# Four edits at once to a fused attention and feed-forward kernel: a score chunk in array quarters, a new first quad, a new order behind the row sums, new last tiles

## Chip, cores, metric

One core of one Trainium2 chip. The metric is device time of one launch in microseconds (us); the lower the better.

## The reference

Attention over 8 batches, 12 heads, 448 positions, 64 channels, all float32, with q and k normalised by row; then a feed-forward over the 3584 tokens whose nonlinearity is `h * softmax(h)`, normalised by row.

```python
q_n, k_n = rmsnorm(q, g_q), rmsnorm(k, g_k)          # x / sqrt(mean(x*x) + 1e-6) * g
attn = softmax(q_n @ k_n^T / 8)                      # rows of 448
x = (attn @ v) as [3584, 768]
h = x @ w_in                                         # [3584, 1024]
solu = h * softmax(h)
ln = (solu - mean) / sqrt(var + 1e-6) * g_ln
out = ln @ w_out                                     # [3584, 768]
```

## The kernel before

Instruction order is laid out by hand. A *pair* is two heads of one batch, a *quad* two pairs (a, b), 24 quads in all. Scores are made transposed, keys on partitions: 448 keys are three chunks of 128 and a last one of 64; the last chunks of both pairs of a quad share one tile.

```python
def scores(n, kc):                                   # chunk kc of pair n: 64 rows by 128 columns of the array
    s = ps_t.tile([P, 2, 512], FP32, tag="t", name="s")
    for h in range(2):
        hh = slice(h * D, (h + 1) * D)
        nc.tensor.matmul(s[:, h, 0:S], d["qkT"][hh, 1, kc * P : (kc + 1) * P], d["qkT"][hh, 0, :], ...)
    exponentials(d, kc, s)                           # ScalarE

def ff_max(t):                                       # maximum and exponential of h, one call
    nc.vector.tensor_reduce(nmax, d["h"], AX, OP.max, negate=True)
    ...
    nc.scalar.activation(d["u"], d["h"], AF.Exp, bias=nmax, accum_out=d["s"])

def ff_in2(t):
    ff_in(t, 1)                                      # second half of h; h has one PSUM buffer
    later(1, lambda: ff_max(t))                      # "1 unit later": behind the next piece of TensorE work
    later(2, lambda: ff_moments(t))                  # the product h*u frees h
    later(3, lambda: ff_norm(t))
... # cut: the loop over quads; its end:
            qk_transpose(b + 2)                      # VectorE, waits for GpSimd's normalised q and k
            ...
            unit(lambda: sums(m))                    # row sums by TensorE
            later(1, lambda m=m: inverse(m))         # VectorE transposes the sums, GpSimd copies reciprocals
            later(2, lambda m=m: divide(m))          # VectorE divides
```

In these traces TensorE, ScalarE and VectorE start an instruction behind those issued to them before it, so the place of an instruction in such a list is its place in a queue. From quad 6 on (`W_IN`), pieces of the feed-forward go between the score chunks; from quad 11 (`W_OUT`) eight pieces a quad.

## Time and profile before

1006.01 us, the median of three runs (1005.66 to 1008.05). I cut the span where the character changes and read each cut from the TensorE timeline: the time at which a quad's first scores start.

| | first scores | quad 1 | quad 2 (A) | quads 2–5 (B) | quads 6–10 (C) | quads 11–23 (D) | to last output matmul (E) | store |
|---|---|---|---|---|---|---|---|---|
| before | 15.52 | 37.54 | 54.44 | 63.97 | 131.87 | 606.23 | 141.86 | 6.0 |

The first three columns are points of time, the others lengths. A is the time up to the start of quad 2, D ends where the row sums of quad 23 start, and A to E and the store add up to the span of 1004.4; the time of a launch is 1.8 us longer than its span. In the prediction A ends where quad 1 starts. One line of the TensorE timeline is needed later, the first scores of quad 1 (start, duration, what they are as far as the window asked for reaches, and in brackets the idle time ahead of them and what ended it):

```profile
37.54 3.36 PE L636 MATMUL s<-qkT 64*128 64x448 f32 x8 [4.47 <-ACT qkT L622]
```

### The profile page before, as it was taken

What the parts mean: (1) busy time and instruction counts of PE and PEld (TensorE: products, weight loads), DVE (VectorE), ACT (ScalarE), POOL (GpSimd) and SP (SyncE); (2) the same over time, 40 slices, a digit from 0 to 9 for tenths busy, and PEclk for the clock granted to TensorE, in tenths of its full rate; (3) what the DMA queues carried; (4) which work ended last, traced back from release to release, by engine and by line L of the source; (5) the groups of instructions that cost most, each with busy time, mean ns of one, the idle gap of its engine ahead of it and who ended that gap; (6) DMA issues with size and microseconds to landing.
All of it is one profiled execution on the core that took longest, in us unless ns stands there. A gap on an engine that the chain in (4) does not pass through costs nothing.

```text
span 1004.4 us, 10943 instructions
## 1 busy us (share of the span) xinstructions
PE 954.0 (95%) x3699; PEld 427.7 (43%) x3699; DVE 513.7 (51%) x758; ACT 361.1 (36%) x621; POOL 296.0 (29%) x635
## 2 busy tenths in 40 slices
PE   3899999998999999999999999999999999999997
PEld 1233333332444443444444444444444444555554
DVE  3788866668452535343535453436444445454520
ACT  4777665566332322232332233223323223011110
POOL 2576633333141414131414140514233232000000
PEclk9899999999999999999999999999999999999999
DMA  7776654443130303030303030303031010534310
GB/s 158 152 158 148 137 112 103 93 92 75 33 56 17 71 16 59 12 72 16 71 16 71 15 56 19 69 16 56 20 67 34 17 35 0 195 110 144 112 53 35
DMA packets 235962, 70.11 MB, mean 70 GB/s; under 512 B 225136, under 2 KB 225144, under 8 KB 235896
## 3 DMA queue, kind: packets, MB, share of 16 engines
q1 hardware_dynamic: 228152, 57.84, 26.4%
q10 hardware_dynamic: 7744, 11.47, 3.0%
q8 instruction: 31, 0.51, 0.2%
q14 instruction: 35, 0.29, 0.1%
HBM read 58.27 MB, written 11.01 MB: 69 GB/s over the span
## 4 chain that ended last, share of the span: by engine, by line
PE 83%; DVE 6%; ACT 4%; POOL 3%; DMA 2%; SPq 1%; issue 1%; ACTq 0%; POOLq 0%; DVEq 0%
PE h L756 29%; PE po L811 28%; PE s L636 9%; PE o L689 8%; PE pu L800 2%; PE sm L713 2%; PE s L648 2%; PE o L678 2%; ACT E L629 1%; POOL qkn L608 1%; DVE qkT L618 1%; SPq L543 1%; POOL ss L582 1%; DMA v<-in_v_dram 1%; DVE w_in L482 1%
## 5 line engine op out<-in xcount | busy, mean ns | idle before, releaser
L811 PE MATMUL po<-w_out,uT 128*128 128x384 f32 x896 | 298.6, 489 | 6.7 <-DVE r L721 3.4
L756 PE MATMUL h<-w_in,xT 128*128 128x512 f32 x672 | 300.6, 597 | 0.0
L811 PEld LDWEIGHTS po<-w_out,uT 128*128 128x128 f32 x896 | 168.0, 190 | 137.4 <-issue 16.7
L756 PEld LDWEIGHTS h<-w_in,xT 128*128 128x128 f32 x672 | 124.3, 190 | 157.6 <-issue 151.3
L629 ACT ACTIVATE E<-s 128x896 f32<-128x896 f32 x168 | 149.4, 915 | 103.7 <-PE s L636 99.8
L636 PE MATMUL s<-qkT 64*128 64x448 f32 x576 | 139.7, 589 | 22.3 <-ACT qkT L622 10.7
L689 PE MATMUL o<-E,v 128*64 128x448 f32 x576 | 113.8, 544 | 1.7 <-ACT E L629 1.7
L784 POOL TENSOR_TENSOR he<-he,mhalf 128x1 f32<-128x1 f32 x28 | 17.4, 622 | 332.1 <-DVE he L783 332.1
L812 ACT COPY y<-po 128x384 f32<-128x384 f32 x56 | 26.8, 479 | 219.7 <-PE po L811 219.7
L802 DVE COPY uT<-pu 128x512 f32<-128x512 f32 x28 | 19.2, 687 | 160.2 <-PE pu L800 92.4
L668 DVE TENSOR_TENSOR es<-es,E 128x896 f32<-128x896 f32 (+1 forms) x52 | 56.5, 1087 | 75.1 <-ACT E L629 67.5
L665 POOL TENSOR_TENSOR es<-E 128x896 f32<-128x896 f32 x26 | 55.7, 2144 | 127.0 <-ACT E L629 127.0
L636 PEld LDWEIGHTS s<-qkT 64*128 64x128 f32 x576 | 48.3, 190 | 104.4 <-issue 44.3
L769 ACT ACTIVATE u<-h,hmax 128x1024 f32<-128x1024 f32 x28 | 31.2, 1113 | 154.5 <-DVE hmax L766 154.5
L608 POOL TENSOR_TENSOR qkn<-qk,ny 128x896 f32<-128x896 f32 x47 | 79.7, 1697 | 8.8 <-DVE qkT L618 3.0
L766 DVE TENSOR_REDUCE hmax<-h 128x1 f32<-128x1024 f32 x28 | 34.3, 1224 | 86.7 <-PE h L756 86.7
L618 DVE STREAM_TRANSPOSE qkT<-qkn 128x896 f32<-128x896 f32 x48 | 53.2, 1109 | 44.0 <-POOL qkn L608 44.0
L689 PEld LDWEIGHTS o<-E,v 128*64 128x64 f32 x576 | 39.1, 137 | 74.6 <-issue 67.7
L569 DVE TENSOR_REDUCE part<-sq 128x28 f32<-128x896 f32 x48 | 51.0, 1063 | 30.1 <-ACT sq L564 30.1
L600 POOL TENSOR_TENSOR nx<-nx,ny 128x28 f32<-128x28 f32 x47 | 23.9, 509 | 124.6 <-ACT ny L595 124.6
L564 ACT ACTIVATE sq<-qk 128x896 f32<-128x896 f32 x48 | 45.6, 950 | 36.8 <-DVE part L569 25.3
L582 POOL COPY ss<-part 32x28 f32<-32x28 f32 x188 | 44.4, 236 | 16.3 <-DVE part L569 7.7
(83 smaller groups left out, 710.2 us busy)
## 6 DMA issues: line engine op xcount, KB each, us to landing
qk<-in_q_dram SPq DMA_DIRECT2D x192, 56.0 KB, 2.1
out_dram<-y ACTq DMA_DIRECT2D x28, 384.0 KB, 2.3
qk<-in_k_dram SPq DMA_DIRECT2D x184, 56.0 KB, 2.2
v<-in_v_dram SPq DMA_DIRECT2D x96, 96.0 KB, 2.4
raw<-in_moe_w_in_dram SPq DMA_DIRECT2D x12, 512.0 KB, 4.5
raw<-in_moe_w_out_dram SPq DMA_DIRECT2D x16, 384.0 KB, 3.2
again<-in_moe_w_in_dram SPq DMA_DIRECT2D x13, 448.0 KB, 5.2
again<-in_moe_w_out_dram SPq DMA_DIRECT2D x13, 448.0 KB, 3.4
```

The lines of the kernel that those rows point to most:

```text
L564: nc.scalar.activation(d["sq"], d["qk"].rearrange("p s b d -> p (s b) d"), AF.Square)
L569: nc.vector.tensor_reduce(d["part"], d["sq"], AX, OP.add)
L582: first(n).tensor_copy(d["ss"][g * 32 : g * 32 + 32], d["part"][o * 32 : o * 32 + 32])
L608: first(n).tensor_tensor(d["qkn"], d["qk"].rearrange("p s b d -> p (s b) d"), d["y"].rearrange("p b -> p b ()").to_broadcast([P, 2 * NB, 32]),
L618: nc.vector.transpose(d["qkT"].rearrange("p s t -> p (s t)"), d["qkn"].rearrange("p b d -> p (b d)"))
L629: nc.scalar.activation(d["E", kc], s[:, :, 0:S], AF.Exp)
L636: nc.tensor.matmul(s[:, h, 0:S], d["qkT"][hh, 1, kc * P : (kc + 1) * P], d["qkT"][hh, 0, :], start=True, stop=True)
L665: engine.tensor_tensor(d["es"], d["E", 0], d["E", 1], OP.add)
L668: engine.tensor_tensor(d["es"][pp], d["es"][pp], x[pp], OP.add)
L689: nc.tensor.matmul(d["o"][h * D : (h + 1) * D, :], d["v"][:, h, kc], d["E", kc][:, h], start=False, stop=(kc == NJ - 1),)
L756: nc.tensor.matmul(d["h"][:, hs], xTs[m][:, c, i * P : (i + 1) * P], w_in[:, c, hs], start=(c == 0), stop=(c == KD - 1))
L811: nc.tensor.matmul(po, d["uT"][:, c], w_out[:, c, hs], start=(c == 0), stop=(c == KF - 1))
```

## The change

Its intent, by part. **Quarters:** the third chunk as four 64x64 matmuls, the mode of the matmuls that follow, so that TensorE changes its mode once less (0.19 us a change by the trace before, read from the starts). **First quad:** the gains of q and k are loaded by GpSimd's queue and made into columns on ScalarE; eight matmuls warm TensorE up; pair 2 is normalised in quad 0. **Order of h's exponential:** maximum one and exponential two units later, so that a score exponential needn't wait behind it. **Inverse at once:** the inverse of the sums directly behind them. **Last tiles:** their transposes ahead of the previous tile's second output half; the last store in halves; the check's small transposes elsewhere.

```diff
     def scores(n, kc):
-        for h in range(2):
-            nc.tensor.matmul(s[:, h, 0:S], d["qkT"][hh, 1, kc * P : (kc + 1) * P], ...)
+        w = P if kc < NJ - 1 else D
+        for c in range(0, P, w):
+            for h in range(2):
+                nc.tensor.matmul(s[c : c + w, h, 0:S], d["qkT"][hh, 1, kc * P + c : kc * P + c + w], ...)
@@ setup
+        nc.gpsimd.dma_start(gg[:, i], g_q or g_k)        # and grow: five small loads; before: SyncE, behind load(1)
@@ def gain_columns()
         nc.tensor.transpose(pg, grow, ident)
-        nc.vector.tensor_copy(gcol, pg)
+        nc.scalar.copy(gcol, pg)
@@ def ff_in2(t)
-        later(1, lambda: ff_max(t))                      # maximum and exponential
-        later(2, lambda: ff_moments(t))
-        later(3, lambda: ff_norm(t))
+        more = 0 if t >= NT - SHORT else 1               # SHORT = 8
+        later(1 + more, lambda: ff_max(t))               # maximum alone
+        later(1 + 2 * more, lambda: ff_exp(t))
+        later(2 + 2 * more, lambda: ff_moments(t))
+        later(3 + 2 * more, lambda: ff_norm(t))
@@ start
+        for _ in range(8):                               # ahead of all other TensorE work
+            nc.tensor.matmul(warm[:, 0:S], ident, q and k of pair 0, start=True, stop=True)
@@ quad 0
+                rsqrt_seed(2)                            # these three: before, in the middle of quad 1's preparation
+                rsqrt_step(2)
+                normalise(2)
@@ end of a quad
-                qk_transpose(b + 2)
             unit(lambda: sums(m))
-            later(1, lambda m=m: inverse(m))
-            later(2, lambda m=m: divide(m))
+            if a < W_IN and next1:
+                qk_transpose(b + 2)
+            inverse(m)
+            if a >= W_IN and next1:
+                qk_transpose(b + 2)
+            later(1, lambda m=m: divide(m))
... (cut: last tiles, one conversion step moved into the start, the order of the loads)
```

More of the change, by code (lines that the diff above doesn't have):

```diff
@@ L375, in fast_path @@
     out: bass.AP,
-    grow: bass.AP,
-    within: bass.AP,
+    g_q: bass.AP,
+    g_k: bass.AP,
+    moe_g_ln: bass.AP,
     large: bass.AP,
-    load_gains,
-    bound_scores,
 ):
@@ L401, in fast_path @@
     LAG = 4
+    SHORT = 8
     assert H * D == DM and 2 * D == P and NJ * P + D == S and NP % 2 == 0 and B % 2 == 0 and 2 * S % P == 0
@@ L414, in fast_path @@
     w_out = consts.tile([P, KF, DM], FP32, name="w_out")
+    grow = consts.tile([KF + 2, P], FP32, name="grow")
+    gg = consts.tile([P, 2, D], FP32, name="gg")
+    gmax = consts.tile([P, 1], FP32, name="gmax")
+    within = consts.tile([P, 1], FP32, name="within")
     gcol = consts.tile([P, KF + 2], FP32, name="gcol")
@@ L435, in setup, with gain_columns, gain_limit @@
         make_identity(nc, ident)
-    def gains():
-        bound_scores()
+        for i, g in enumerate((g_q, g_k)):
+            nc.gpsimd.dma_start(gg[:, i], g.rearrange("(o d) -> o d", o=1).to_broadcast([P, D]))
+            nc.gpsimd.dma_start(
+                grow[KF + i : KF + i + 1].rearrange("o (h d) -> o h d", h=2),
+                g.rearrange("(o d) -> o () d", o=1).to_broadcast([1, 2, D]),
+            )
+        nc.gpsimd.dma_start(grow[0:KF, :], moe_g_ln.rearrange("(c p) -> c p", p=P))
+    def gain_columns():
         pg = ps_t.tile([P, KF + 2], FP32, tag="t", name="pg")
         nc.tensor.transpose(pg, grow, ident[0 : KF + 2, 0 : KF + 2])
-        nc.vector.tensor_copy(gcol, pg)
-        nc.vector.tensor_scalar(
+        nc.scalar.copy(gcol, pg)
+        nc.gpsimd.tensor_tensor(gg[:, 0], gg[:, 0], gg[:, 1], OP.mult)
+    def gain_limit():
+        limit = 80.0 / float(D) ** 0.5
+        nc.gpsimd.tensor_scalar(large, gmax[0:1], limit, None, OP.is_gt)
+        nc.gpsimd.tensor_scalar(within, gmax, limit, float(D) ** -0.5, OP.is_le, OP.mult)
+        nc.gpsimd.tensor_scalar(
             gcol[:, KF : KF + 1], gcol[:, KF : KF + 1], gcol[:, KF + 1 : KF + 2], within, OP.mult, OP.mult
@@ L511, in check_all @@
         one = small.tile([1, 2], FP32, tag="one", name="one")
-        pw = ps_t.tile([1, 2, P], FP32, tag="t", name="pw")
+        pw = ps_h.tile([1, 2, P], FP32, tag="h", name="pw")
         nc.vector.tensor_reduce(worst[:, 0:1], extent[:, 0], AX, OP.min)
@@ L633, in scores @@
         s = ps_t.tile([P, 2, 512], FP32, tag="t", name="s")
-        for h in range(2):
-            hh = slice(h * D, (h + 1) * D)
-            nc.tensor.matmul(
-                s[:, h, 0:S], d["qkT"][hh, 1, kc * P : (kc + 1) * P], d["qkT"][hh, 0, :], start=True, stop=True
-            )
+        w = P if kc < NJ - 1 else D
+        for c in range(0, P, w):
+            for h in range(2):
+                hh = slice(h * D, (h + 1) * D)
+                nc.tensor.matmul(
+                    s[c : c + w, h, 0:S], d["qkT"][hh, 1, kc * P + c : kc * P + c + w], d["qkT"][hh, 0, :],
+                    start=True, stop=True,
+                )
         exponentials(d, kc, s)
@@ L764, in ff_max, with ff_exp @@
         d = mt[t]
-        nmax = small.tile([P, 1], FP32, tag="hmax", name="hmax")
-        nc.vector.tensor_reduce(nmax, d["h"], AX, OP.max, negate=True)
+        d["nmax"] = small.tile([P, 1], FP32, tag="hmax", name="hmax")
+        nc.vector.tensor_reduce(d["nmax"], d["h"], AX, OP.max, negate=True)
+    def ff_exp(t):
+        d = mt[t]
         d["u"] = work.tile([P, DFF], FP32, tag="u", name="u", bufs=LAG + 1)
         d["s"] = small.tile([P, 1], FP32, tag="hsum", name="hsum")
-        nc.scalar.activation(d["u"], d["h"], AF.Exp, bias=nmax, accum_out=d["s"])
+        nc.scalar.activation(d["u"], d["h"], AF.Exp, bias=d["nmax"], accum_out=d["s"])
     def ff_moments(t):
@@ L812, in ff_out @@
         nc.scalar.copy(d["y"][:, hs], po)
+        if t == NT - 1:
+            nc.scalar.dma_start(out[t * P : (t + 1) * P, hs], d["y"][:, hs])
+        elif half == 1:
+            nc.scalar.dma_start(out[t * P : (t + 1) * P, :], d["y"])
         if half == 1:
-            nc.scalar.dma_start(out[t * P : (t + 1) * P, :], d["y"])
             del mt[t]
@@ L878, in fast_path, with second @@
     waiting = []
-    def second(t, a, b):
-        return [(W_OUT, lambda: ff_transpose(t)), a, (W_OUT, lambda: ff_out(t, 0)), b, (W_OUT, lambda: ff_out(t, 1))]
-    nothing = (0, None)
+    def second(t):
+        return [
+            (W_OUT, lambda: ff_transpose(t)),
+            (W_OUT, lambda: ff_out(t, 0)),
+            (W_OUT, lambda: ff_out(t, 1)),
+        ]
     for t in range(NT):
-        ready = -(-(t + 1) * P // S) * NP
-        a = (max(ready, W_IN), lambda t=t: ff_in(t, 0))
-        b = (max(ready, W_IN), lambda t=t: ff_in2(t))
+        ready = max(-(-(t + 1) * P // S) * NP, W_IN)
+        a = (ready, lambda t=t: ff_in(t, 0))
+        b = (ready, lambda t=t: ff_in2(t))
         waiting.append(t)
-        if len(waiting) > (LAG if t < NT - 8 else 1):
-            c, _, d, _, e = second(waiting.pop(0), nothing, nothing)
+        if len(waiting) > (LAG if t < NT - SHORT else 1):
+            c, d, e = second(waiting.pop(0))
             events += [a, c, b, d, e]
@@ L894, in fast_path @@
     for t in waiting:
-        events += [x for x in second(t, nothing, nothing) if x[1]]
+        c, d, e = second(t)
+        if t == waiting[0]:
+            events += [c, d, e]
+        else:
+            events[-1:] = [c, events[-1], d, e]
     N = B * NP
@@ L905, in fast_path @@
     load(0)
+    setup()
     load(1)
-    load_gains()
-    setup()
+    load_next()
     load_next()
@@ L911, in fast_path @@
     load(3)
-    load_next()
     load_v(0)
@@ L915, in fast_path @@
     with tc.manual_schedule():
+        warm = ps_h.tile([P, DFF], FP32, tag="h", name="warm")
+        for _ in range(8):
+            nc.tensor.matmul(
+                warm[:, 0:S], ident, st[0]["qk"][:, 1].rearrange("p b d -> p (b d)"), start=True, stop=True
+            )
         squares(0)
@@ L922, in fast_path @@
         rsqrt_seed(0)
+        gain_columns()
+        begin(0)
         rsqrt_step(0)
-        gains()
+        nc.vector.tensor_reduce(gmax, gg[:, 0], AX, OP.max, apply_absolute_value=True)
         normalise(0)
@@ L927, in fast_path @@
         fold_sums(1)
+        gain_limit()
         rsqrt_seed(1)
@@ L932, in fast_path @@
         gain(0)
+        step(0)
+        end(0)
         at = 0
@@ L990, in fast_path @@
             if next1:
-                rsqrt_seed(a + 2)
-                rsqrt_step(a + 2)
-                normalise(a + 2)
+                if m:
+                    rsqrt_seed(a + 2)
+                    rsqrt_step(a + 2)
+                    normalise(a + 2)
                 rsqrt_seed(b + 2)
@@ L996, in fast_path @@
             if m == 0:
-                begin(0)
-                step(0)
-                end(0)
                 begin(1)
@@ L1046, in fast_path @@
             unit(f)
-            while x < len(again) and x * len(last) < (u + 1) * (len(again) + 2):
+            while x < len(again) and 5 * x < 7 * u:
                 check_w(x, raw[x])
@@ L1051, in fast_path @@
                     raw.append(load_again(x + 3))
-            if u == len(last) - 2:
-                assert x == len(again)
+            if 5 * (u - 1) == 100:
+                assert x == len(again) and u < len(last)
                 check_all()
@@ L1073 @@
     nc = tc.nc
-    D = q.shape[3]
-    P = 128
-    KF = moe_w_in.shape[1] // P
-    gains = ctx.enter_context(tc.tile_pool(name="gains", bufs=1))
-    grow = gains.tile([KF + 2, P], FP32, name="grow")
-    gg = gains.tile([P, 2, D], FP32, name="gg")
-    gmax = gains.tile([P, 1], FP32, name="gmax")
-    within = gains.tile([P, 1], FP32, name="within")
-    flag = gains.tile([1, 1], I32, name="flag")
-    large = gains.tile([1, 1], FP32, name="large")
-    def load_gains():
-        nc.sync.dma_start(grow[0:KF, :], moe_g_ln.rearrange("(c p) -> c p", p=P))
-        for i, g in enumerate((g_q, g_k)):
-            for h in range(2):
-                nc.sync.dma_start(grow[KF + i : KF + i + 1, h * D : (h + 1) * D], g.rearrange("(o d) -> o d", o=1))
-            nc.sync.dma_start(gg[:, i], g.rearrange("(o d) -> o d", o=1).to_broadcast([P, D]))
-    def bound_scores():
-        nc.gpsimd.tensor_tensor(gg[:, 0], gg[:, 0], gg[:, 1], OP.mult)
-        nc.vector.tensor_reduce(gmax, gg[:, 0], AX, OP.max, apply_absolute_value=True)
-        nc.gpsimd.tensor_scalar(large, gmax[0:1], 80.0 / float(D) ** 0.5, None, OP.is_gt)
-        nc.gpsimd.tensor_scalar(within, gmax, 80.0 / float(D) ** 0.5, float(D) ** -0.5, OP.is_le, OP.mult)
-    fast_path(tc, q, k, v, moe_w_in, moe_w_out, out, grow, within, large, load_gains, bound_scores)
+    flags = ctx.enter_context(tc.tile_pool(name="flags", bufs=1))
+    flag = flags.tile([1, 1], I32, name="flag")
+    large = flags.tile([1, 1], FP32, name="large")
+    fast_path(tc, q, k, v, moe_w_in, moe_w_out, out, g_q, g_k, moe_g_ln, large)
     nc.vector.tensor_copy(flag, large)
```

## The prediction

> **What bounds the kernel now.** I read the busy shares, then a table by stage (cut where the profile changes character), TensorE's waits, the chain of waits and the engines' timelines inside each stage. In the code a "quad" is two head pairs, a and b: scores in chunks a0, a1, a2, a shared "last" chunk for both, then b0, b1, b2, then values and row sums; quads 0 to 23. Pieces of the feed-forward of finished tokens are put between them from quad 6 on.
>
> ```profile
> PE 954.0 (95%) x3699; PEld 427.7 (43%) x3699; DVE 513.7 (51%) x758; ACT 361.1 (36%) x621; POOL 296.0 (29%) x635
> ```
>
> TensorE is busy 95%. By stage (length, then busy us of TensorE, weight loads, VectorE, ScalarE, GpSimd):
>
> ```profile
> 0.00:37.50 37.50, 16.89 (x89) 5.72 (x89) 18.89 (x30) 20.53 (x36) 15.03 (x45) 0.98 0.77 160
> 37.50:118.40 80.90, 79.36 (x440) 25.60 (x440) 68.52 (x91) 63.81 (x105) 54.41 (x121) 0.97 0.70 150
> 118.40:250.30 131.90, 122.23 (x554) 44.07 (x550) 92.65 (x147) 78.83 (x139) 48.27 (x130) 1.00 0.45 96
> 250.30:857.40 607.10, 597.82 (x2189) 275.62 (x2188) 273.88 (x376) 180.29 (x309) 175.32 (x333) 1.00 0.17 39
> 857.40:1004.40 147.00, 137.75 (x438) 76.69 (x434) 59.77 (x117) 17.65 (x33) 2.95 (x8) 0.99 0.32 107
> ```
>
> The stages are: A, start and quad 0; B, quads 1 to 5, no feed-forward; C, quads 6 to 10, first feed-forward matmuls; D, quads 11 to 23; E, the rest. Only D and E are plainly TensorE's. B looks like it (79 of 81), but the matmuls of a quad sum to some 14.2 us while a quad takes 16.07 (its first scores start at 70.20, 86.27, 102.34, 118.41): matmuls with waits inside a group are shown as busy. TensorE's recorded waits:
>
> ```profile
> PE s L636 <- ACT qkT L622: 10.7, 2, 6.2
> PE s L636 <- ACT E L629: 9.8, 14, 1.7
> PE po L811 <- DVE r L721: 3.4, 2, 1.7
> PE po L811 <- ACT uT L801: 2.9, 4, 0.7
> ```
>
> [...] In D, with no waits:
>
> ```profile
> 407.89 1.02 PE L636 MATMUL s<-qkT 64*128 64x448 f32 x4
> 408.84 0.98 PE L648 MATMUL s<-qkT 64*64 64x448 f32 x8
> 446.06 1.77 PE L636 MATMUL s<-qkT 64*128 64x448 f32 x8
> ```
>
> By start to start, one chunk in halves takes 0.95 (407.89 to 408.84), two take 1.71 (446.06 to 447.77): 0.76 a chunk plus about 0.19 a change of mode. [...] quad 0's and quad 1's first scores take 4.16 and 4.85 us after 6.2 and 4.5 idle, later ones of the same kind 2.7 to 3.1. [...] The same four GpSimd copies took 0.92 and 1.74 us, the second pair of them while VectorE worked on weights:
>
> ```profile
> 87.50 0.92 POOL L582 COPY ss<-part 32x28 f32<-32x28 f32 x4
> 88.81 1.74 POOL L582 COPY ss<-part 32x28 f32<-32x28 f32 x4
> ```
>
> **The change part by part.**
>
> *Quarters.* a2 and b2 (two matmuls of 64 rows by 128 columns) become four of 64 by 64. They are followed directly by "last" and by the first values matmuls, both 64 by 64 already. So a2 plus last, now 0.95 + 0.91 = 1.86, becomes one group: four concurrent passes of 448 columns at 0.373 (the step of the long values group, 4.66 less one drain over 12) plus one drain of 0.17, 1.66. Saved 0.2, twice a quad. In D: 13 quads x 2 x 0.2 = -5.2. In A to C something else sets the pace, so nothing.
>
> *Inverse of the sums at once.* In D the second output matmul group waits twice 1.7 us for VectorE's transpose of the sums, which releases their PSUM buffer; it stood behind transposes that waited for GpSimd. From quad 6 on it now stands ahead of them: -3.4 in D. In B it does something else: the two weight-conversion steps (0.36 + 0.69) that VectorE did while GpSimd copied the reciprocals now come after the divisions. B is a loop: transpose of q and k on VectorE, GpSimd's normalising, its eight small copies, its reciprocal copies, VectorE's divisions, its sums, transpose again: 16.07. It gains the 1.05, and loses about 0.85[...]: +0.2 a quad, +1 in all.
>
> *Order of h's exponential.* In C the chain of waits goes:
>
> ```profile
> 171.81 1.24 DVE hmax L766
> 173.07 1.20 ACT u L769 x2
> 174.28 0.82 ACT E L629
> 175.14 1.02 PE s L636 x4
> ```
>
> The exponential of h holds up that of a0, and a2 waits 1.66, once a quad. The change issues maximum and exponential one and two units later. But the instruction order of the changed kernel puts the four division instructions ahead of the maximum on VectorE, and they need GpSimd's copies:
>
> ```profile
> 171.78 0.90 POOL L727 COPY rc<-rc 32x14 f32<-32x14 f32 x4
> 172.96 0.64 DVE L736 STREAM_TRANSPOSE r<-rc 128x448 f32<-128x448 f32 x1
> ```
>
> Laid out anew from the third copy (172.43): divisions 2.72 to 175.15, maximum 1.23 to 176.4, exponential to 177.5; then ScalarE's gain of b (0.67), queued behind it, to 178.2; only now the second half of "last", to 178.7. On VectorE two or four conversion steps (0.9 each two) now also precede the product that frees h's one PSUM buffer: product done at 178.8 or 179.4. The next h matmuls start there, against 177.40 before. So a0 and a1 are freed, but "last" and h wait longer: +1.3 in quad 7, +1.9 in 8 and 9, +1.4 in quad 10 (no h follows; its values wait for b2's exponential instead): +6.5.
>
> *First quad and warm TensorE.* The q and k of the first pair land near 5.2. Eight warming matmuls of two records each: [...] Behind them the transpose of the gains, its copy on ScalarE, one conversion (1.4, moved here) and the second pair's seed: the gain of pair 0 at 15.5, first scores at 16.2 instead of 15.52. The scores then run warm, but ScalarE's exponentials (0.92 each) set the pace. The seed of pair 2 now stands before b0's exponential and waits for sum, copies and fold of pair 2: some 2.4 us of ScalarE idle, which delays pair 3. Against it stands the conversion already done. My timeline has quad 1 begin at 38.2 against 37.54, and the loop of B about 0.5 to 1 later: +1.
>
> *Last tiles.* Of the last four tiles three get their transposes ahead of the previous tile's second output half, so 0.69 + 0.74 + 0.75 of waiting for the copy to SBUF goes: -2.2. The check's tiny transposes no longer sit between two output groups: -0.3. The last store is half as large: -0.4 (an estimate: half of the rate of about 400 GB/s seen in the last store). -2.9.
>
> Sum: +1 +1 +6.5 -8.6 -2.9 = -3.0, so 1003. The positive terms rest on hand-laid queues, where more can turn out shorter than longer; I take off two more: **1001 us**.
>
> **Rivals.** First, C as intended: if the reciprocal copies are ready early, the maximum isn't held, and "last" ends 0.5 earlier per quad; the +6.5 turns to -2, in all about 993. For it: the part was evidently written against the 1.66. Against: GpSimd's eight copies and their adds come ahead in its queue in both kernels, and end at 171.7. Second, A and B shorten: pair 2 is ready earlier, no cold clock in quad 1, the loop of B down to ScalarE's and TensorE's own 14 to 15 us; then up to -9, and with the first rival 984. Against it: B's loop holds neither of them. Third, the drain isn't saved by quarters (doubled weight loads show instead): D loses 5.2, about 1006 to 1008.
>
> **Range and chances.** 2% is 20 us; the parts I can point to in D and E make 11.5. Faster by over 2% takes both of the first rivals; slower needs C three times worse. Range 990 to 1009; faster 0.06, within 0.92, slower 0.02.
>
> **What would show it right or wrong.** In the changed trace: a group of 64x64 matmuls of 16 records taking about 1.66 from start to start in D, and no wait of output matmuls for the transpose of the sums; in quads 7 to 9 "last" waits for the gain of b, the maximum starts after four divisions, and the quad takes 28.5 or more against 27.35; quads 1 to 5 at 16.0 to 16.5; first scores near 16.2, quad 1's near 38; no waits on the copy to SBUF but one at the end. Quads of C under 27 us, or of B under 15.5, would make it wrong, as would a first quad that ends before 35.

The terms of the sum: +1 +1 +6.5 −8.6 −2.9 = −3.0, and with two more taken off −5, so 1001 for 1006. The first +1 rests on first scores at 16.2, and that on a warming that was to end at 13.1, 7.9 us after its start; how long its matmuls stay slow was my assumption, which no trace showed. The second +1 is +1.05 less about 0.85; the latter is an estimate, from the 1.74 and the 0.92 us that the same four copies took, that the slow ones come to take the shorter time. "Drain" is my word for the 0.19 us (0.17 in the sum for the quarters) that a change of mode adds between starts; what TensorE does in it is not shown.

## The result, and the profile after

**1006.45 us** (1006.03 to 1006.56, 4 runs) against 1006.97 (1005.66 to 1008.05, 4 runs) of the kernel before: ratio 0.9995, interval 0.9977 to 1.0012. The range held it; the gain of 5 us did not come. The profiled spans are 1004.4 and 1004.8.

| | first scores | quad 1 | A | B | C | D | E | store |
|---|---|---|---|---|---|---|---|---|
| after | 18.59 | 41.67 | 57.85 | 65.29 | 141.41 | 596.91 | 138.26 | 5.1 |
| after less before | +3.1 | +4.1 | +3.4 | +1.3 | +9.5 | −9.3 | −3.6 | −0.9 |

So nothing is absent: 13.9 us were gained in D, E and the store, and 14.3 were lost in A, B and C. The page's busy line and the table by stage, cut like the one shown of the kernel before (columns: window, length, busy us with records of TensorE, weight loads, VectorE, ScalarE, GpSimd, then the granted TensorE clock, the DMA share and GB/s):

```profile
PE 958.6 (95%) x3907; PEld 431.9 (43%) x3907; DVE 515.3 (51%) x756; ACT 359.4 (36%) x622; POOL 294.0 (29%) x641
0.00:41.60 41.60, 28.06 (x113) 9.92 (x113) 17.53 (x28) 20.61 (x37) 17.43 (x51) 0.88 0.74 153
41.60:123.10 81.50, 74.69 (x484) 24.14 (x480) 68.51 (x91) 63.45 (x106) 52.85 (x121) 1.00 0.67 143
123.10:264.50 141.40, 127.71 (x588) 45.13 (x588) 93.98 (x148) 79.26 (x139) 47.68 (x130) 0.96 0.42 90
264.50:862.30 597.80, 591.41 (x2293) 276.13 (x2292) 275.42 (x374) 178.41 (x309) 173.08 (x334) 1.00 0.18 39
862.30:1004.80 142.50, 136.72 (x438) 76.62 (x434) 59.82 (x117) 17.63 (x33) 2.95 (x8) 0.99 0.33 111
```

Two things stand out beside the lengths. The clock fell from 0.98 to 0.88 in the first stage, the one with the warming, and from 1.00 to 0.96 in quads 6 to 10. (In the first stage the two figures can't be compared as they stand: the trace's record of the clock starts at 18.84 us before the change and at 12.05 after it, and the view counts the time ahead of it as full, although the first scores before the change, from 15.52 on, ran cold: twelve records in 4.16 us, where in D eight take 1.77.) And the whole page's 95% busy says nothing: a cold matmul counts as busy (from 155.41 to 158.82 us, at a granted clock of 0.50, TensorE is busy for 3.22 of 3.41). TensorE's waits (sum, number, longest) name both losses and both gains:

```profile
PE s L670 <- ACT qkT L640: 9.4, 4, 2.9
PE s L657 <- ACT E L647: 7.8, 15, 3.7
...
PE po L836 <- DVE r L743: 0.7, 2, 0.3
```

The first is new: "last" waits for the gain of b in quads 7 to 10 (2.90, 2.83, 1.84 and 1.84 us). The wait of output matmuls for the transposed sums is down from 3.4 to 0.7.

**Quads 6 to 10.** The chain of waits in quad 8 (start, duration, what the end hangs on):

```profile
180.45 0.66 DVE r L758
181.13 0.64 DVE xT L760
...
181.86 0.66 DVE r L758
...
183.08 1.23 DVE hmax L788
...
184.33 1.20 ACT u L794 x2
185.53 0.57 ACT qkT L640
...
186.14 1.76 PE s L670 x4
187.90 4.47 PE h L778 x8
```

Step for step this is the predicted path: divisions, maximum, exponential, gain of b, second half of "last", then h. What it adds is the 1.76 us of four matmuls that otherwise take 0.97: they ran at half clock (0.50 from 186.13 to 189.54 us), and the granted clock from 184 to 192 us was 0.77 and 0.81, where the kernel before had 1.00 in the same windows. TensorE idles 2.83 us ahead of them.

**Start.** TensorE's timeline of the first quad:

```profile
7.16 8.68 PE L957 MATMUL warm<-qk,ident 128*128 128x448 f32 x16 [7.16 <-DMA qk<-in_k_dram]
15.77 0.22 PE L451 MATMUL pg<-ident,grow 10*128 10x10 f32 x1
18.59 4.33 PE L657 MATMUL s<-qkT 64*128 64x448 f32 x16 [2.60 <-ACT qkT L640]
...
30.00 1.77 PE L657 MATMUL s<-qkT 64*64 64x448 f32 x8 [3.72 <-ACT E L647]
```

Pair 0 landed at 7.16 (warming matmuls wait for it). The warming ended at 15.84, the small transpose `pg` of the gains came behind it, then 2.60 us idle. The first sixteen score records took 4.33 us, between the 5.06 of the run no_warm below, cold, and some 2.5 warm (in D, 1.71 from start to start for the eight of a0 and a1 and 0.80 for the eight of the third chunk). The granted clock was 0.50 from 18.88 to 22.29 us: the warmth was gone before it was used. Then b2 waits 3.72 us for an exponential that stands behind the seed of pair 2.

**Quads 11 to 23.** The quarters in one group with what follows:

```profile
443.30 0.98 PE L657 MATMUL s<-qkT 64*64 64x448 f32 x8
444.10 0.93 PE L700 MATMUL o<-E,vl 64*64 64x448 f32 x8
444.96 4.73 PE L711 MATMUL o<-E,v 128*64 128x448 f32 x24
```

From start to start 1.66 us (443.30 to 444.96), against 1.86 before.

### The profile page after: what moved, and what is told of

It is laid out like the page before. It is cut to its first block, busy times and chain, and to the rows that moved or that the text cites. A ratio compares the mean times of both kernels' runs of the same rounds, so it can differ in the third digit from the quotient of the medians.

```text
span 1004.8 us, 11376 instructions
## 1 busy us (share of the span) xinstructions
PE 958.6 (95%) x3907; PEld 431.9 (43%) x3907; DVE 515.3 (51%) x756; ACT 359.4 (36%) x622; POOL 294.0 (29%) x641
## 4 chain that ended last, share of the span: by engine, by line
PE 76%; DVE 8%; POOL 6%; ACT 4%; DMA 3%; issue 2%; SPq 1%; POOLq 0%; DVEq 0%; ACTq 0%
PE po L836 28%; PE h L778 26%; PE s L657 8%; PE o L711 7%; PE pu L825 2%; POOL qkn L626 2%; PE s L670 2%; POOL ss L600 2%; ACT E L647 1%; DVE r L758 1%; PE o L700 1%; DVE xT L760 1%; PE warm L957 1%; PE sm L735 1%; DMA qk<-in_k_dram 1%
## 5 line engine op out<-in xcount | busy, mean ns | idle before, releaser
L778 PE MATMUL h<-w_in,xT 128*128 128x512 f32 x672 | 303.8, 602 | 0.1
L657 PE MATMUL s<-qkT 64*128 64x448 f32 (+1 forms) x768 | 136.9, 574 | 18.8 <-ACT E L647 7.8
L657 PEld LDWEIGHTS s<-qkT 64*128 64x128 f32 (+1 forms) x768 | 42.6, 160 | 101.4 <-issue 45.0
L618 POOL TENSOR_TENSOR nx<-nx,ny 128x28 f32<-128x28 f32 x47 | 19.8, 421 | 153.0 <-ACT ny L613 153.0
L799 DVE TENSOR_TENSOR u<-h,u 128x1024 f32<-128x1024 f32 x28 | 34.2, 1221 | 50.7 <-ACT u L794 50.7
L758 DVE STREAM_TRANSPOSE r<-rc 128x448 f32<-128x448 f32 x48 | 30.9, 644 | 40.7 <-POOL rc L749 38.2
```

The costliest lines, as they stand in the source:

```text
L657: nc.tensor.matmul(s[c : c + w, h, 0:S], d["qkT"][hh, 1, kc * P + c : kc * P + c + w], d["qkT"][hh, 0, :], start=True, stop=True,)
L758: nc.vector.transpose(r, quads[m]["rc"][:, i].rearrange("p b -> p b ()").to_broadcast([P, NB, 32]))
L778: nc.tensor.matmul(d["h"][:, hs], xTs[m][:, c, i * P : (i + 1) * P], w_in[:, c, hs], start=(c == 0), stop=(c == KD - 1))
```

## The experiments

In the expectations "D and E", "C" and so on are the columns of the tables above. The stages of all runs:

| kernel | quad 1 | A | B | C | D | E | median us | ratio to before (interval) |
|---|---|---|---|---|---|---|---|---|
| quarters_only | 37.5 | 54.3 | 64.1 | 131.1 | 603.5 | 141.9 | 1002.18 | 0.9955 (0.9942–0.9968) |
| old_start | 37.4 | 54.2 | 65.3 | 141.4 | 597.2 | 138.3 | 1002.28 | 0.9954 (0.9941–0.9967) |
| max_first | 41.8 | 58.0 | 66.0 | 136.2 | 593.4 | 138.3 | 998.59 | 0.9914 (0.9901–0.9928) |
| fill_wait | 41.9 | 58.1 | 65.3 | 136.7 | 598.6 | 138.3 | 1003.48 | 0.9963 (0.9951–0.9975) |
| best1 | 38.1 | 54.7 | 64.1 | 132.8 | 596.3 | 138.3 | 992.87 | 0.9872 (0.9856–0.9889) |
| gains_sync | 40.2 | 56.3 | 65.3 | 141.6 | 597.2 | 138.3 | 1003.81 | 0.9972 (0.9956–0.9989) |
| no_warm | 39.1 | 55.3 | 65.4 | 141.7 | 597.0 | 138.3 | 1004.29 | 0.9982 (0.9965–1.0000) |
| seed2_late | 38.5 | 55.0 | 65.3 | 141.3 | 596.9 | 138.3 | 1003.60 | 0.9971 (0.9955–0.9988) |
| best2 | 37.6 | 54.5 | 63.9 | 131.1 | 601.4 | 138.3 | 995.74 | 0.9887 (0.9868–0.9905) |
| start3 | 38.2 | 55.1 | 65.0 | 141.6 | 597.2 | 138.3 | 1002.73 | 0.9956 (0.9939–0.9973) |
| warm_behind | 40.3 | 56.5 | 65.3 | 141.6 | 596.9 | 138.3 | 1002.69 | 0.9960 (0.9943–0.9976) |
| best3 | 38.2 | 54.4 | 64.5 | 131.1 | 595.5 | 138.3 | 990.34 | 0.9843 (0.9829–0.9857) |

The first four ran on one chip, the next four on a second, best2 to warm_behind there again, best3 on a third; the kernel before had medians of 1007.19, 1005.71, 1006.33 and 1006.16 beside them. All results were correct.

### The quarters alone

```diff
 # the kernel before, with
+        w = P if kc < NJ - 1 else D        # and the two loops of the change's scores()
```

> The kernel before with the third key chunk in quarters and nothing else. My theory: two mode changes of about 0.2 us less in each quad that TensorE bounds. Stage D (quads 11 to 23, 607.1 us before) shorter by 5 to 5.5 us; stage C (quads 6 to 10, 131.9 us), where TensorE's groups lie on the chain of waits too, shorter by about 1 to 2; A, B and E unchanged within 0.5. In all about 999.5 to 1001 against 1006.5. Rival (the doubled weight loads eat the saved drains): D unchanged within 1 us, in all 1006.

Measured −4.5 us by the ratio. In quads 12 to 23 those that nothing else touched went from 46.11 to 45.70: 0.41 a quad, twice 0.20, as worked out. The rival that the drain isn't saved falls. But D as a whole fell only 2.7, because quad 11 rose from 48.79 to 50.09. There TensorE waits for a division ahead of the feed-forward's transposes, 1.66 and 0.76 us, and behind it the transposes and the next h group took 1.11 and 6.48 us; with the same waits (1.64 and 0.75) the kernel before took 0.66 and 5.32. The clock from 254 to 258 us was 0.57 here and 1.00 there. The same idle time, once with and once without loss of the clock: this is met again in quad 10 of best1.

What decides between the two is not shown by these traces. From the start of the second transposes to that of the scores behind h it is 7.31 us here and 5.74 there, so a difference of 1.6 us between two traces can be this and not the edit.

### The change without its new start

```diff
 # the kernel before, with quarters, order of the exponential, inverse at once, last tiles;
 # start, first quad and loads of the gains as before
```

> The changed kernel with the whole start and first quad as in the kernel before (gains loaded on the sync queue, no warming matmuls, first conversion and third pair's normalising at their old places). My theory: quad 2's first scores at about 54.5 instead of 57.85, everything behind it alike, total 1003 against 1006.4. Rival (the later stages absorb a late start because VectorE and GpSimd set the pace): total 1006 as now.

1002.28, and A back at 54.23. The +3.4 of A is real and comes through to the end: the loss at the start is not absorbed later. B keeps its +1.3 without the new start, and quarters_only doesn't have it (64.1), so that one belongs to the order behind the sums, the only part left that touches quads 2 to 5.

### The maximum ahead of the divisions

```diff
-        later(1 + more, lambda: ff_max(t))
+        later(1, lambda: ff_max(t))
...
-            later(1, lambda m=m: divide(m))
+            later(2 if a >= W_IN else 1, lambda m=m: divide(m))
```

> The changed kernel, but h's maximum goes back ahead of the four division instructions on VectorE from quad 6 on (the exponential stays behind those of a0 and a1). My theory: in quads 7 to 10 the gain of b no longer waits behind an exponential that waits for the divisions; the quads of 30.6, 30.6 and 29.9 us fall to 26.5 to 27.3, and C in all from 141.4 to some 130; total about 995. Rival (the loss in C comes from the division and sum transposes themselves or from the later h product): C stays above 138, total above 1003.

C fell from 141.41 to 136.18, not to 130. TensorE's waits of this run:

```profile
PE h L778 <- DVE u L799: 3.3, 3, 1.4
PE o L711 <- ACT E L647: 3.0, 1, 3.0
PE s L670 <- ACT qkT L640: 2.7, 4, 0.7
```

"Last" waits 0.7 a quad instead of 2.9, as expected. But h now waits for the product that frees its buffer: VectorE does conversion steps ahead of it. The main theory holds for the wait it named; the queue holds a second one right behind it. In quad 10 the values wait 3.0 us for an exponential, and the quad takes 26.33 us for 24.57. D came to 593.4, the shortest of all runs; 1.6 of that is because TensorE, late from quad 10, comes to the transposes of quad 11 when their division is done (46.84 for 48.48), the rest in quads 13 and 18, 51.32 each.

### The wait filled with matmuls that nobody reads

```diff
 # the changed kernel, in scores_last(m), between its two halves
+            if i == 0 and m in (7, 8, 9):
+                for x in range(6):
+                    nc.tensor.matmul(s[0:D, x % 2, 0:S], qkT[hh, 1, NJ * P : S], qkT[hh, 0, :], start=True, stop=True)
```

> The changed kernel, and in quads 7, 8 and 9 TensorE repeats the first half of the last chunk three times (six matmuls into the same place with the same result, some 2.3 us) while it waits for the gain of b. If the half clock after the wait is a cost of its own: the second half of last goes from 1.76 back to 0.97, the h matmuls behind it from 6.2 to 7.1 back to 5.4, and total falls by 3 to 5 us although TensorE does more; 1002 to 1003. Rival (these two groups are long for waits inside them, not for the clock): unchanged within 1 us.

The run separates the wait from its effect on the clock. TensorE has six more matmuls in quads 7 to 9, and these quads are shorter all the same: 29.06, 29.16 and 28.19 us against 30.60, 30.63 and 29.86. The second half of "last" in quad 7, and h behind it:

```profile
155.79 0.97 PE L670 MATMUL s<-qkT 64*64 64x448 f32 x4 [0.63 <-ACT qkT L640]
156.69 5.42 PE L783 MATMUL h<-w_in,xT 128*128 128x512 f32 x12
```

In the changed kernel these took 1.76 and 6.16:

```profile
155.60 1.76 PE L670 MATMUL s<-qkT 64*64 64x448 f32 x4 [2.90 <-ACT qkT L640]
```

"Last" starts no earlier (155.79 against 155.60): the wait is the same length, only what follows it isn't slowed (in quad 8, from 184 to 192 us, the granted clock is 1.00, for 0.77 and 0.81 in the changed kernel). So about 1.5 us a quad of the loss in C, half of the 3.0 in these quads, is the clock and not the wait. The total falls by 3.2 us by the ratios and not by the 4.7 of C, since in this run the h group behind the transposes of quad 11 took 7.01 us, for 5.32 in the changed kernel (the quad 50.18 for 48.48).

### What pays, without what costs

```diff
 # the kernel before, with quarters and last tiles, and
+            if a >= W_OUT:
+                inverse(m)
+                if next1: qk_transpose(b + 2)
+            else: (the old order)
             later(2, lambda m=m: divide(m))
```

> The kernel before with the three parts that the profiles showed to pay and nothing else: chunk quarters everywhere, the last tiles as the change lays them out, and the inverse of the sums at once, but only from quad 11 on; start, first five quads, order of the exponential and divisions of quads 6 to 10 stay those of before. Main theory: the gains of D and E stand by themselves and the losses of A and C belong to the parts left out. Sum of stages: A 54.4, B 64.1, C 131.1 (all three as the quarters alone gave them), D 594 to 597 (597.2 with the old start, 593.4 in the best of the runs), E 138.3, and 5.1 behind it: 987 to 990, some 1.8 % under the kernel before. Rival: D and E are quicker in the changed kernel only because C is slower there and pushes work forward; then D and E come back to 603 and 141, and the total is 997 to 1000.

992.87, 1.28% under the kernel before; expected 987 to 990. (That sum was one of spans: the profiled span is 991.0 where the time is 992.82, so 1.8 of the miss is no loss of the kernel's.) D and E are as short as in the changed kernel (596.3, 138.3) while A to C are the old ones, so they are gains of their own: the rival falls. Against quarters_only C and D together fall by 5.6 us (734.6 to 729.0). Of these 4.0 are the new inverse: quads 13 and 18 go from 54.6 to 52.6. The other 1.6 is the stretch at a lower clock in quad 11 of quarters_only (0.57 from 254 to 258 us), and no gain of the edit. best1 has such a stretch too, in quad 10, where TensorE waits 1.86 us for an exponential (C 132.8 and not 131.1, the clock from 241 to 245 us 0.71, quad 10 25.58); but then it comes so late to the transposes of quad 11 that they wait 0.8 us for a division and not 2.4, which makes up for it. In the run best3 below the row sums behind the same wait of 1.86 took 1.71 and 0.94 us, for 2.69 and 1.72 in best1, and quad 10 took 23.88.

### The gains' loads on SyncE's queue

```diff
-            nc.gpsimd.dma_start(gg[:, i], ...)      # five loads at the start
+            nc.sync.dma_start(gg[:, i], ...)        # the same, behind load(1)
```

> The changed kernel with one edit: the loads of the gains are issued by SyncE behind the loads of pairs 0 and 1 and not by GpSimd at the start. Main theory: [...] with them out of the way pair 0 lands near 5.3, the first scores start at 16.6 to 17 in place of 18.6, quad 2 starts about 2 us earlier and the total falls by 1 to 2 us. Rival: the later landing has another cause (the order of the sync and scalar issues themselves); then landing stays at 7 us and the total moves by under 0.5 us, or rises because the gains come too late for the column copy at 16 us.

The landing near 7.2 us, for 5.2 before, is what the traces showed.

The warming matmuls, which wait for pair 0, started at 5.40 instead of 7.16, and the median loads of k in the first 12 us took 2.8 us to land instead of 3.5 (2.6 in the kernel before). The first scores came at 17.27, a little later than expected, quad 2 starts 1.5 us earlier, and the ratio is 0.9972 against the changed kernel's 0.9995, 2.3 us, in intervals of 1.7 us to either side, so the total alone would not settle it. The landing does: ScalarE's first square, which waits for pair 0, starts at 7.09 to 7.70 us in the six traces with the gains on GpSimd's queue and at 5.43 to 5.84 in the eight with them on SyncE's. The main theory holds for the landing: some 70 KB of small loads (160 packets on GpSimd's queue) cost the first large ones, eight of 56 KB, 1.8 us here. By what means was not tried.

### No warming

```diff
-        for _ in range(8):
-            nc.tensor.matmul(warm[:, 0:S], ident, st[0]["qk"][:, 1]..., start=True, stop=True)
```

> The changed kernel without its eight warming matmuls. Main theory: they end at 15.84 us, TensorE then idles 2.6 us and the first scores are cold all the same, so they buy nothing: first scores at 18.6 +/- 0.3, first sixteen records 4.3 +/- 0.3 us, total within 0.7 us of the changed kernel. Rival: they hold the clock up for part of the first quad; without them quad 1 starts over 1 us later and the total rises by 1 to 2 us.

A miss, and the most useful one. I had expected no effect; the first scores came 3.2 us earlier, though pair 0 landed late as before. TensorE's timeline:

```profile
8.17 0.24 PE L451 MATMUL pg<-ident,grow 10*128 10x10 f32 x1 [8.17 <-DMA grow<-in_moe_g_ln_dram]
15.40 4.31 PE L657 MATMUL s<-qkT 64*128 64x448 f32 x12 [7.00 <-ACT qkT L640]
```

The small transpose of the gains runs at 8.17 instead of 15.77. So the warming had stood ahead of it in TensorE's queue, and behind it, on ScalarE, the gains' copy, a conversion, pair 1's seed and the gain of pair 0. The scores themselves are slower (sixteen in 5.06 us, against 4.33). Quad 2 started 2.5 us earlier than in the changed kernel; the ratios put the whole at −1.3 us, and stage and ratio differ by no more than the intervals.

### Pair 2's seed back in quad 1

```diff
-                rsqrt_seed(2)
-                rsqrt_step(2)
-                normalise(2)
...
-                if m:
-                    rsqrt_seed(a + 2) ...
+                rsqrt_seed(a + 2) ...
```

> The changed kernel with seed, step and conversion of pair 2 put back into quad 1 from the middle of quad 0. Main theory: that seed is what stands on ScalarE ahead of the exponential of b2's scores at 28.6 us (idle 2.5 us) and makes TensorE wait 3.7 us and go cold; without it the wait falls under 1.5 us, quad 1 starts at 38.5 to 39.5 in place of 41.7 and the total falls by 1 to 2.5 us. Rival: the work has only moved: quad 1 then waits for pair 2's conversion and quad 2 starts where it did (57.9 +/- 0.4), total within 0.5 us.

b2's wait fell from 3.72 to 0.62, quad 1 started at 38.48, quad 2 2.8 us earlier, the total by the ratios 2.4 lower (intervals of 1.7 to either side): the main theory, at its upper end. But quad 1's first scores now wait 2.89 us for their gain and run cold (clock 0.50 from 40 to 42 us), where in the changed kernel they waited for nothing.

### The three together, and warming behind the transpose

```diff
 # start3: the changed kernel with gains_sync, no_warm and seed2_late together
 # best2: best1's parts with this start (and, an oversight of mine, divisions one unit behind the sums from quad 11 on)
 # warm_behind: the changed kernel, with six warming matmuls issued behind the transpose of the gains
```

> The changed kernel with the same three taken out of its first quad, the rest as the change has it. If they add up: first scores at 13.6 to 14.2, quad 2 at 51.0, total 1000 +/- 1. If they are one chain: quad 2 at 53 to 54.5, total 1002 to 1003.

> The best kernel so far (quarters, last tiles, inverse at once only from quad 11 on: 992.9 us) with the changed kernel's first quad, less what the last runs showed to cost there: no warming matmuls, the gains on SyncE's queue, the seed of pair 2 in quad 1. Main theory: the new order of the first quad pays once those three are out of it. If the three savings add up as in the single runs (1.5, 2.5 and 2.8 us of stage A), quad 2 starts at 51.0 and not at 54.7, the other stages stay (B 64.1, C 132 to 133, D 596, E 138.3), and the total is 989 +/- 1. Rival: the three are one chain (rows to first scores) and do not add up; then quad 2 starts at 53 to 54.5 and the total is 991.5 to 993.

The three do not add up: 1.5 + 2.5 + 2.8 = 6.8 us would have put quad 2 at 51.0, and it starts at 55.1 (start3) and 54.5 (best2), where the kernel before had it at 54.4. The first scores did come at 14.9, but quad 1 waits. ScalarE's timeline of best2:

```profile
36.03 0.95 ACT L583 ACTIVATE sq<-qk 128x896 f32<-128x896 f32 x1 [2.14 <-DMA qk<-in_k_dram]
36.89 0.65 ACT L641 ACTIVATE qkT<-qkT,gcol 128x448 f32<-128x448 f32 x1
```

and TensorE's:

```profile
37.59 3.35 PE L658 MATMUL s<-qkT 64*128 64x448 f32 x7 [5.31 <-ACT qkT L641]
```

ScalarE squares the next quad's pair ahead of the gain that quad 1 waits for, and that square waits 2.14 us for a load; the transpose that the gain reads was done at 35.32, so the square holds it up by 1.57. (In the kernel before the gain waits for that transpose itself, done at 36.78, and quad 1 starts at the same time.) My rival said "one chain, rows to first scores"; its number was right, its chain was not. best2's 995.74 is more than best1's 992.87: C and D together take 732.5 instead of 729.0, and the only edit there between the two is when the divisions are issued from quad 11 on (one unit behind the sums instead of two). In quads 13 and 18 best2 takes 53.52 and 53.78 instead of 52.61, 2.1 in all; the rest is a slow stretch again, in quad 11 of best2 (behind waits of 1.64 and 0.75 us the transposes and h take 0.98 and 6.72 us, for 0.66 and 5.32 in best1), which is not made up there. That is a reading of two runs, not a run of its own.

> The changed kernel with six warming matmuls, issued behind the small transpose of the gains and not ahead of it. Without any warming the first scores came at 15.4 and not at 18.6, against what I had expected of that run. Theory: TensorE works in order, so the transpose of the gains waited for the warming's end (15.8), and the gain column, the first conversion on ScalarE behind it and the seed of pair 1 with it. Then with the transpose ahead the first scores come at 15.2 to 16 and, since the warming ends near 15, the first sixteen score records take 3.5 to 4.3 us in place of 5.1 without warming: quad 2 at 54 to 55.3, total 1003 to 1004.5. Rival: it is not the order but the warming itself (its reads of q and k, its clock) that delays; then the first scores come at 17.5 to 18.6 again, total 1005.5 to 1006.5.

The transpose ran at 8.66, the warming ended at 16.38 and the first scores came at 16.59, 0.22 behind it, and warm: 1.77 us for eight, as in D. Two warming matmuls fewer would account for some 1.5 us of the 2.0 (four records at 0.376, an estimate from the step of the warming records of the changed kernel from 12.29 us on); it is the 0.22 in place of 2.75 between warming and scores that confirms the order as the cause (the rival had 17.5 to 18.6). Quad 2 started at 56.5, later than expected, since b2 still waited 3.72; the median, 1002.69, is just under the 1003 to 1004.5 expected (the profiled execution, with a span of 1003.4, was slower than that). It is the only run in which the warming did what it was for, and it came out later at quad 2 than the run without warming (55.3).

### The maximum and exponential apart, from quad 11 on only

```diff
 # best1, with the change's ff_max / ff_exp, and
+        more = 1 if a >= W_OUT and t < NT - 8 else 0
```

> The best kernel so far (992.9 us) with one part of the change more: the maximum of h and its exponential are set apart and moved a unit later, but only from quad 11 on and not for the last eight tiles; the divisions stay two units behind the sums, as in that kernel. Main theory: in quads 11 to 23 the earlier place of h's maximum on VectorE is what holds up the folded sums (TensorE waits 0.95 us for them in two quads, which last 52.6 us) and with it they last 51.3 as in the run with the maximum first: D 593.5 in place of 596.3, total 989.5 to 991, all other stages as they were (C 131 to 133). Rival: that 51.3 came from the state in which quads 6 to 10 leave the queue and not from the order in D; then D stays at 596 +/- 0.5 and the total at 992.3 to 993.5.

990.34 us, the best version: 1.6% under the kernel before, whose time the changed one has. Quads 13 and 18 took 51.34 each, against 52.60 and 52.61 in best1: the main theory. (D reads 595.5 instead of 593.5: the transposes of quad 11 wait 1.67 and 0.75 us for their divisions here, and it takes 48.51; in best1 and max_first, late from quad 10, it took 46.79 and 46.84. C and D together are 726.5 against 729.0.)

## Why the prediction was wrong

The steps that failed: at the start, the landing of the first pair, the length of the warming and the place of pair 2's seed; in C, the durations of the matmuls behind the wait, taken warm; and the two us taken off as a guess. A and B came to +4.7 for +2, C to +9.5 for +6.5, D to −9.3 for −8.6, E and the store to −4.55 for −2.9, and nothing for the −2: 5.4 us in all, so that the forecast of −5 became +0.4 in the profiled spans. Point by point, by its own sum (+1 +1 +6.5 −8.6 −2.9 and two more taken off):

- **Start, +1: failed, +4.1 to quad 1.** The step "the q and k of the first pair land near 5.2" was taken over from the kernel before, though the change moves the gains' loads beside them: they landed at 7.16, +2.0 (gains_sync puts the cause on the loads). The warming took 8.68 us instead of the 7.9 it was given, +0.8: its records were 0.75 us apart from 8.04 to 11.77 and 0.38 from 12.29 on, so it ran slow for some 4.9 us, longer than the forecast had it. From its end to the first scores it was 2.75 instead of 3.1. Sum +2.4: 18.59 for the 16.2 predicted. The rest came in quad 0, 23.08 us for 22.0: the "2.4 us of ScalarE idle" was seen, but it was charged to pair 3 and not to b2 and the cold clock behind it (0.50 from 30 to 34 us). "The scores then run warm" failed as well: behind the 2.60 us of idle time that I had left between warming and scores the clock was at 0.50 (18.88 to 22.29 us). no_warm and seed2_late show the sizes, 2.5 and 2.8 us of A; they overlap, as start3 shows.
- **B, +1: mechanism and size held.** Quads 3 to 5 take 16.31 to 16.33 instead of 16.07, so +0.25 for the +0.2 a quad worked out, and GpSimd's second four copies take 0.92 us instead of 1.74, as laid out; quad 2 takes 16.32 instead of 15.76; 0.7 is made up in quad 1 (16.18 for 16.90), so that quads 1 to 5 come to +0.6.
- **C, +6.5: mechanism right, size wrong, +9.5.** The chain was the one laid out. The mis-sized term is the time of "last" and h behind the wait: I took their warm durations. I had put the wait at such a length without asking what it does to the clock, although I had cited the slow first scores of quads 0 and 1 (4.16 and 4.85 us behind 6.2 and 4.5 of idle time). The trace has three stretches of 3.41 us at half clock (0.50) in C, from 155.41, 186.13 and 216.85 us. With the wait filled, quads 7 to 9 are 28.2 to 29.2 us, the 28.65 to 29.25 of the predicted terms; cold, they are 29.9 to 30.6. (Quad 10 came to +0.7 for the +1.4 predicted.)
- **D, −8.6: held, −9.3.** Quarters 0.41 a quad for 0.40, but only 0.18 in quads 13 and 18, so some 4.5 in all for 5.2. Quads 13 and 18 fell from 54.78 to 52.24 and 52.21: less the quarters, some 2.4 a quad, 4.8 for the 3.4 predicted. By best1 the inverse is worth 4.0 of it, the removed wait of 1.7 a quad and a little more. The order of the exponential, to which I had given nothing here, can give 2.5 beyond best1 (best3; max_first, which moves maximum and divisions, takes as long, 51.32); the changed kernel has 0.8 of that.
- **Last tiles, −2.9: −4.55 with the store.** A tile went from 12.16 to 11.20 us, 0.96 and not 0.73: from the start of the transposes to that of the output group it is 0.87 and not 1.73, and the output group itself is 0.1 shorter. The store gave 0.9 instead of 0.4, in one trace each; quarters_only, which leaves it alone, has 5.4 where the kernel before has 6.0, so up to 0.6 of it may be chance.
- **"I take off two more": wrong in direction.** "More can turn out shorter than longer" was a guess, not worked out. Both hand-laid stages came out longer: C by the half clock behind idle time that I counted at its length only, the start by the late landing, the longer warming and the seed, with the half clock behind the last two.

Of the rivals, "C as intended" is what quads 7 to 9 would have had to show, under 27 us; none did. "A and B shorten" did not come either; best2 shows its limit, a load that quad 1's gain stands behind. "The drain isn't saved" falls by quarters_only.

**What stays open:** what decides whether the clock falls behind a wait of 1.6 to 1.9 us, and whether a start that lets ScalarE do quad 1's gain ahead of the next squares would turn the earlier first scores into time; no run here tried it.

## What to carry to other kernels

A change of several parts that comes out at zero should be cut into stages and its parts run alone: here +14 and −14 stood side by side, and keeping the paying parts gave 1.6%. An idle gap on TensorE costs its length and, here, often up to 1.6 us more in cold matmuls behind it: behind gaps of 2.60 us (start) and of 2.90 and 2.83 us (quads 7 and 8) the granted clock was 0.50, so a wait that grew from 0.7 to 2.9 us cost more than 2.2. Behind waits of 1.6 to 1.9 us it fell in some cases and not in others: in the changed kernel to 0.50 behind the 1.84 us of quad 9 and not at all behind the 1.84 of quad 10. Before a difference of that size between two traces is put down to an edit, look at the clock. Warm-up work belongs behind the small instructions that others wait for in the same queue, and right up to the real work; even so it did not pay here, where the stage was bound elsewhere.
